# Independent list scatters with waiting readers, and the last block's partial sums loaded ahead

## The chip, the cores and the metric

The kernel runs on one core of one Trainium2 chip. The time is the device time of one execution in microseconds (us); a verdict compares medians of several executions.

## What is computed

Three stages, all in float32, over 2304 tokens of 512 columns: an attention (4 batches, 8 heads, 576 positions, 64 columns a head) with a threshold on the scores; a dense two-layer block with leaky ReLU and 2048 hidden columns; and a mixture of 8 experts in which every token goes to the one expert that its logits choose.

```python
x = attention(q, k, v, tau).transpose(0, 2, 1, 3).reshape(2304, 512)
h = x @ w_in
x = np.maximum(0.01 * h, h) @ w_out
logits = x @ w_gate + modality_bias[modality_id]
e_idx = np.argmax(logits, axis=1)
for e in range(8):
    mask = e_idx == e
    h = np.maximum(x[mask] @ w1[e], 0.0)          # 1024 hidden columns
    out[mask] = gate_w[mask, None] * (h @ w2[e])  # gate_w: the softmax of the chosen logit
```

## The kernel before, in words

A float32 matrix is split into a high and a low part, and a product is three matmuls (high x high, high x low, low x high). The program is one fixed order of instructions for each engine, written out by Python generators; nothing is scheduled by a planner. Each engine works its own row in order, and the framework adds the waits between engines and for DMAs from what reads and writes what.

The attention (0 to about 545 us) works 128 rows at a time; in its gaps the `Units` compute the first 6 of the 16 hidden slices of the dense block for blocks of 256 tokens, and write these partial sums to DRAM (`yp`). There are 9 blocks (`NB`). After the attention, `Tail.run` goes through a list of `items`, each one hidden slice (128 columns) of one block or group: first layer into `h` (L421), activation, and two items later (`LAG` is 2) the second layer into `y` (L453). The items are: slices 0 to 5 of blocks 6 to 8; slices 6 to 15 of the blocks in pairs (0 and 1, 2 and 3, 4 and 5, 6 and 7); slices 6 to 15 of block 8 alone; then two early expert groups of 8 slices each. What has to be done ahead of an item stands in a list `pre` with the item's number at which it falls due: loads of tokens (`fetch`), loads of partial sums (`fetch_part`), transposes (`turn`), and for the early groups `ahead` with the loads of ids and weights, the gather of the group's tokens and the splits of its weights.

When a block's last slice is through, `done1` adds the partial sums to `y` and puts steps for that block into `extra`, of which a few run per item: logits, expert choice and rank (`Route.block`), then three DMAs on POOL: the tokens with their gate to DRAM (`yd`, L604), and two scatters of 128 token numbers each (L606) into `idt`, the lists of the experts. Both scatters write the same DRAM tensor; the framework takes the second as one that overwrites the first, and lets POOL wait for the first to land. For the pairs of blocks the partial sums are loaded ahead into the buffers `xgs`; for block 8 they are loaded in `done1` itself, straight into the buffer of the result.

After 6 blocks `early` picks the first two groups: the 256 first tokens of the two fullest experts. `load_ids` loads a group's numbers from `idt` on SP, `gather` clamps them on VectorE (L881) and lets POOL fetch the token rows (L883) into `xgs`. After block 8, `table` sorts the rest of the tokens into groups of 256 or 384 and singles. `Groups.first` loads the first of these dynamic groups (list L1059 and weights L1075, L1077 on SP, gather L1065 on POOL) while the early groups run; then come dynamic loops over groups, each with the loads for the next.

In the rows, PE is TensorE, DVE VectorE, ACT ScalarE, POOL GpSimd, SP the engine that issues most loads. `h`, `y`, `tp` and `ytp` are accumulators, `w` split weights, `cr`, `ur`, `raw` and `eraw` buffers for raw weights, `g` activations, `exg` the gathered tokens of a dynamic group, `eid` its list.

Of the kernel before, what the change touches and what calls it, by code (L numbers as in the profile page):

```python
# [11 lines left out]
F32 = mybir.dt.float32  # L12
# [443 lines left out]
class Route:  # L456
    def __init__(self, tc, cp, dram, ident, mid, wg, wgt, mb, tmp):
# [10 lines left out]
        self.have = 0  # L468
# [92 lines left out]
    def block(self, b, y, sb, ps, ps_tag):  # L561
# [43 lines left out]
        for t in range(2):  # L605
            nc.gpsimd.indirect_dma_start(out=self.idt, out_offset=IOA(ap=pi[:, t:t + 1], axis=0),  # L606
                                         in_=self.ids[:, 2 * b + t:2 * b + t + 1], in_offset=None)
            yield

# [134 lines left out]
class Tail:  # L744
# [83 lines left out]
    def fetch_part(self, b):  # L828
        for t in range(2):
            self.tc.nc.sync.dma_start(self.xgs[b % 2][:, t, 0:DM], self.mo.yp[2 * b + t])  # L830

    def done1(self, b, ys, part):
        nc = self.tc.nc
        yt = self.yt()
        for t in range(2):
            if part == 2:
                nc.vector.tensor_tensor(yt[:, t, 0:DM], ys[t], self.xgs[b % 2][:, t, 0:DM], op=ALU.add)
            elif part:
                nc.sync.dma_start(yt[:, t, 0:DM], self.mo.yp[2 * b + t])
                nc.vector.tensor_tensor(yt[:, t, 0:DM], ys[t], yt[:, t, 0:DM], op=ALU.add)  # L840
            elif t == 0:
                nc.vector.tensor_copy(yt[:, t, 0:DM], ys[t])
            else:
                nc.scalar.activation(yt[:, t, 0:DM], ys[t], AF.Copy)
# [27 lines left out]
    def load_ids(self, g):  # L872
        assert self.blocks == NB - 3
        base = self.entry(g, 1, NID - GT)
        ids = self.idb()
        self.tc.nc.sync.dma_start(ids, self.rt.idt[ds(base, GT), :].rearrange("(p t) o -> p (t o)", t=2))
        self.ids[g] = ids
# [46 lines left out]
    def ahead(self, g, p):  # L924

        a = [(0, 0, lambda: self.load_ids(g)), (p - 7, 1, lambda: self.gather(g)),
# [103 lines left out]
class Groups:  # L1030
# [25 lines left out]
    def load_ids(self, slot, to, nt=3):  # L1056
        nc = self.nc
        base = nc.sync.value_load(self.rt.slot(1, slot), min_val=0, max_val=NID - TT)
        nc.sync.dma_start(to[:, 0:2], self.rt.idt[ds(base, GT), :].rearrange("(p t) o -> p (t o)", t=2))  # L1059
# [318 lines left out]
def body(tc, qkt, vt, tau, win, wout, mid, wg, wgt, mb, w1, w2, out):  # L1378
    nc = tc.nc
    with ExitStack() as top, tc.manual_schedule():  # L1380
# [73 lines left out]
        def both(b, ys):  # L1454
            for k in range(2):
                ta.done1(b + k, ys[2 * k:2 * k + 2], 2)
# [9 lines left out]
        pre += [(p - 4, 0, 0, lambda: ta.fetch(b))] + [(p - 2 + t, 0, 0, lambda t=t: ta.turn(b, t)) for t in range(2)]  # L1466
        items += [item(b, fi, start=fi == NA, stop=fi == NF - 1, done=(lambda ys: ta.done1(b, ys, 1))) for fi in range(NA, NF)]
# [91 lines left out]
```

## Time and profile before

| | |
|---|---|
| median of 3 runs | 1040.73 us (1039.37 to 1041.92) |
| the profiled execution | 1042.11 us, of it span 1040.3 us |
| TensorE matmul busy | 934.5 us (90%), 7073 instructions |
| weight loads of TensorE | 818.0 us (79%) |
| VectorE busy | 716.6 us (69%) |
| ScalarE busy | 590.6 us (57%) |
| GpSimd busy | 433.6 us (42%) |
| mean granted TensorE clock | 0.958 of full speed |

TensorE is the busiest engine, with an average that mixes stages: some 475 of the first 545 us, nearly all of the time from 545 to 754 us, with gaps between 754 and 811 us, and again nearly all of it until 992 us. The span is counted from the first to the last instruction; what lies around it is 1.8 us. A row that says what an engine waited for names the one event that came last.

### The profile page before, as it was taken

Reading aid. Unit: us, or ns where it says so; the run is one execution under the profiler, and the core shown is the slowest. Engines: PE = TensorE matmul, PEld = TensorE weight load, DVE = VectorE, ACT = ScalarE, POOL = GpSimd, SP = SyncE. Lnnn points to the kernel's source line nnn. Section 1 sums busy time; section 2 is a strip of 40 time slices with the busy share of each in tenths; the row PEclk is TensorE's granted clock in tenths of the full one; section 3 lists DMA queues with packets and bytes.
Section 4 is the critical chain, followed back from the end, with each engine's and each line's share of the span. In section 5 each row is a group of like instructions: output and inputs, shape, how many; then the busy total and the mean of one; then the engine's idle time right before and its main releaser. Section 6 shows DMA issues by size and latency. Waiting matters only on the chain. (4 is left out here: it accounts for less than half of the span.)

```text
span 1040.3 us, 20475 instructions
## 1 busy us (share of the span) xinstructions
PE 934.5 (90%) x7073; PEld 818.0 (79%) x7073; DVE 716.6 (69%) x1749; ACT 590.6 (57%) x1168; POOL 433.6 (42%) x523
## 2 busy tenths in 40 slices
PE   4666779999998998999999999999978999999993
PEld 3565769888897997887887878788967898998962
DVE  7988989889898984776247473844656666565573
ACT  6687878889897874664222222222524555664473
POOL 3899988889888872332001010010122211221120
PEclk7888899999999998999999999999989999999997
DMA  8899999999999986554040220124694987766472
GB/s 214 212 210 255 224 231 205 206 213 240 222 200 216 214 158 181 181 183 142 1 162 20 48 75 20 61 41 143 100 195 135 342 298 260 250 227 202 128 275 104
DMA packets 261721, 181.96 MB, mean 175 GB/s; under 512 B 186258, under 2 KB 223254, under 8 KB 261592
## 3 DMA queue, kind: packets, MB, share of 16 engines
q1 hardware_dynamic: 249248, 155.78, 60.6%
q0 software_dynamic: 6032, 17.68, 5.9%
q10 hardware_dynamic: 6312, 6.94, 2.2%
q8 instruction: 61, 1.00, 0.5%
q14 instruction: 68, 0.56, 0.2%
HBM read 118.88 MB, written 19.79 MB: 133 GB/s over the span
## 5 line engine op out<-in xcount | busy, mean ns | idle before, releaser
L196 POOL TENSOR_TENSOR p<-p,p 128x512 f16<-128x512 f32 x144 | 170.3, 1182 | 0.0
L150 PE MATMUL s<-khh,qs 128*128 128x288 f32 x320 | 104.9, 342 | 49.8 <-DVE p L175 27.9
L453 PE MATMUL y<-w,g 128*128 128x512 f32 x480 | 130.7, 409 | 0.0
L429 ACT ACTIVATE ct<-h 128x256 f32<-128x256 f32 (+1 forms) x104 | 48.5, 466 | 139.7 <-PE h L421 135.2
L158 DVE TENSOR_REDUCE s<-s 128x1 f32<-128x576 f32 x144 | 109.3, 759 | 26.4 <-PE s L223 23.0
L431 DVE SCALAR_TENSOR_TENSOR h<-h,ct 128x256 f32<-128x256 f32 (+1 forms) x104 | 55.2, 531 | 104.8 <-ACT ct L429 104.5
L175 DVE SCALAR_TENSOR_TENSOR p<-s,tb,e 128x576 f32<-128x576 f32 x144 | 117.2, 814 | 8.3 <-ACT e L167 5.2
L421 PE MATMUL h<-w,w 128*128 128x512 f32 x480 | 120.3, 396 | 1.3 <-ACT w L410 0.9
L453 PE MATMUL y<-w,w 128*128 128x512 f32 x480 | 119.2, 395 | 0.0
L222 PE MATMUL s<-vs,pt 128*128 128x128 bf16 (+1 forms) x680 | 109.0, 228 | 5.9 <-DMA pt<-p 5.9
L150 PEld LDWEIGHTS s<-khh,qs 128*128 128x128 f32 x320 | 66.2, 207 | 58.7 <-DVE p L175 18.3
L167 ACT ACTIVATE e<-s,tb 128x576 f32<-128x576 f32 x144 | 107.2, 744 | 4.6 <-DVE tb L162 4.5
L421 PEld LDWEIGHTS h<-w,w 128*128 128x128 f32 x480 | 89.2, 188 | 22.9 <-ACT w L410 1.3
L453 PEld LDWEIGHTS y<-w,w 128*128 128x128 f32 x480 | 88.9, 188 | 19.1
L223 PE MATMUL s<-vs,pt 128*128 128x64 bf16 (+1 forms) x680 | 104.0, 198 | 0.0
L194 ACT ACTIVATE p<-p 128x576 f16<-128x576 f32 x144 | 99.3, 690 | 5.1 <-DVE tb L162 4.2
L453 PEld LDWEIGHTS y<-w,g 128*128 128x128 f32 x480 | 86.2, 192 | 14.6
L150 PE MATMUL s<-kll,qs 128*128 128x288 f32 x320 | 96.4, 315 | 0.0
L421 PE MATMUL h<-uxh,w 128*128 128x256 f32 x448 | 90.5, 300 | 3.2 <-DVE g L440 2.5
L225 PE MATMUL s<-vs,pt 128*128 128x128 bf16 (+1 forms) x544 | 89.8, 226 | 0.0
L421 PE MATMUL h<-exh,w 128*128 128x256 f32 (+1 forms) x448 | 85.8, 288 | 0.7 <-ACT exh L410 0.7
L222 PEld LDWEIGHTS <-pt 128*128 128x128 f16 (+1 forms) x680 | 68.9, 104 | 18.2 <-DMA pt<-p 7.3
(250 smaller groups left out, 2286.7 us busy)
## 6 DMA issues: line engine op xcount, KB each, us to landing
cr<-w SPq DMA_DIRECT2D x36, 512.0 KB
raw_qk<-qkt SPq DMA_DIRECT2D x30, 576.0 KB
raw<-w SPq DMA_DIRECT2D x24, 512.0 KB
eraw<-w SPq DMA_DIRECT2D x18, 512.0 KB
cr<-w_in SPq DMA_DIRECT2D x16, 512.0 KB
cr<-w_out SPq DMA_DIRECT2D x16, 512.0 KB
ur<-xd SPq DMA_DIRECT2D x13, 512.0 KB
ur<-w SPq DMA_DIRECT2D x12, 512.0 KB
```

The source lines that it names most:

```text
L150: nc.tensor.matmul(s[:, j, 0:288], qf[:, c0:c0 + P], x[:, j * 288:(j + 1) * 288], start=(k == 0), stop=(k == len(ops) - 1))
L158: v.tensor_reduce(self.mq[n], self.sq[n], axis=AX.XY, op=ALU.min)
L167: self.tc.nc.scalar.activation(e, self.sq[n], AF.Exp, bias=self.mq[n][:, 1:2], scale=-1.0)
L175: self.tc.nc.vector.scalar_tensor_tensor(p, self.sq.pop(n), self.mq.pop(n)[:, 0:1], self.eq.pop(n), op0=ALU.is_le, op1=ALU.mult, accum_out ...
L194: nc.scalar.activation(pp[:, 0:S], p, AF.Copy)
L196: nc.gpsimd.tensor_tensor(pp[:, S + D:], p[:, 0:4 * P], pp[:, 0:4 * P], op=ALU.subtract)
L222: nc.tensor.matmul(o[r0:r1, 0:2 * D], hi, v12, start=(c == 0), stop=False)
L223: nc.tensor.matmul(o[r0:r1, D:2 * D], hi, vs[:, h, c, 2], start=False, stop=(c == 4))
L225: nc.tensor.matmul(o[r0:r1, 0:2 * D], pt[:, 5 + c, r0:r1], v12, start=False, stop=False)
L421: nc.tensor.matmul(h, w[:, 0, a, s], b[:, c], start=(n == 0), stop=(n == 11))
L431: nc.vector.scalar_tensor_tensor(h, h, 0.01, a, op0=ALU.mult, op1=ALU.max)
L453: nc.tensor.matmul(y, a[:, s], w[:, 1, b], start=start and k == 0, stop=stop and k == 2)
```

## The change

Four edits. `fetch_part` and `done1`: block 8's partial sums go into the buffer `xgs[1]` too, by an entry in `pre` due five items into block 8, and `done1` has one form for all blocks. `Route.block`: the 18 scatters are declared to be independent of one another, their names are kept in `put`, and a memset of one column follows each on POOL. `listed`: the loads of lists in `load_ids` (both of that name) wait for all scatters issued so far. `ahead`: a group's gather is due one item later.

```diff
@@ -465,7 +465,8 @@
         nc.scalar.dma_start(bs, mb.rearrange("(o m) e -> o m e", o=1).to_broadcast([P, 2, E]))
         mi = tmp[4].bitcast(I32)[:, 0:36].rearrange("p (t w) -> p t w", w=2)
         nc.scalar.dma_start(mi, mid.bitcast(I32).rearrange("(t p) w -> p t w", p=P))
-        self.have = 0
+        self.have, self.put = 0, []
+        self.gap = cp.tile([P, 1], F32, name="gap")
         self.consts = self.prepare(nc, cp, dram, tmp, bs, mi)
 
     def prepare(self, nc, cp, dram, tmp, bs, mi):
@@ -603,9 +604,19 @@
         v.tensor_copy(pi, pf)
         nc.gpsimd.dma_start(self.yd[b * GT:(b + 1) * GT, :].rearrange("(t p) c -> p t c", t=2), y)
         for t in range(2):
-            nc.gpsimd.indirect_dma_start(out=self.idt, out_offset=IOA(ap=pi[:, t:t + 1], axis=0),
-                                         in_=self.ids[:, 2 * b + t:2 * b + t + 1], in_offset=None)
+            i = nc.gpsimd.indirect_dma_start(out=self.idt, out_offset=IOA(ap=pi[:, t:t + 1], axis=0),
+                                             in_=self.ids[:, 2 * b + t:2 * b + t + 1], in_offset=None)
+            self.tc.declare_no_dep(i.ins, group="idt", reason="every token has its own place in the lists")
+            self.tc.add_to_no_dep_group("idt", i.ins)
+            self.put.append(i.ins.name)
+            nc.gpsimd.memset(self.gap, 0.0)
             yield
+
+    def listed(self, dma):
+
+        for name in self.put:
+            self.tc.add_manual_dep(dma.ins, name, mybir.DependencyInfo(mybir.DependencyClass.Sync, mybir.DependencyReason.DATA))
+        self.put = []
 
     def early(self, sb):
 
@@ -826,22 +837,15 @@
             self.tc.nc.scalar.dma_start(self.mo.yp[2 * b + t], o)
 
     def fetch_part(self, b):
+        to = self.xgs[b % 2 if b < NB - 1 else 1]
         for t in range(2):
-            self.tc.nc.sync.dma_start(self.xgs[b % 2][:, t, 0:DM], self.mo.yp[2 * b + t])
-
-    def done1(self, b, ys, part):
+            self.tc.nc.sync.dma_start(to[:, t, 0:DM], self.mo.yp[2 * b + t])
+
+    def done1(self, b, ys):
         nc = self.tc.nc
         yt = self.yt()
         for t in range(2):
-            if part == 2:
-                nc.vector.tensor_tensor(yt[:, t, 0:DM], ys[t], self.xgs[b % 2][:, t, 0:DM], op=ALU.add)
-            elif part:
-                nc.sync.dma_start(yt[:, t, 0:DM], self.mo.yp[2 * b + t])
-                nc.vector.tensor_tensor(yt[:, t, 0:DM], ys[t], yt[:, t, 0:DM], op=ALU.add)
-            elif t == 0:
-                nc.vector.tensor_copy(yt[:, t, 0:DM], ys[t])
-            else:
-                nc.scalar.activation(yt[:, t, 0:DM], ys[t], AF.Copy)
+            nc.vector.tensor_tensor(yt[:, t, 0:DM], ys[t], self.xgs[b % 2 if b < NB - 1 else 1][:, t, 0:DM], op=ALU.add)
         if self.blocks == 0:
             self.rt.load_wide(self.raws[2:])
         self.blocks += 1
@@ -873,7 +877,7 @@
         assert self.blocks == NB - 3
         base = self.entry(g, 1, NID - GT)
         ids = self.idb()
-        self.tc.nc.sync.dma_start(ids, self.rt.idt[ds(base, GT), :].rearrange("(p t) o -> p (t o)", t=2))
+        self.rt.listed(self.tc.nc.sync.dma_start(ids, self.rt.idt[ds(base, GT), :].rearrange("(p t) o -> p (t o)", t=2)))
         self.ids[g] = ids
 
     def gather(self, g):
@@ -923,7 +927,7 @@
 
     def ahead(self, g, p):
 
-        a = [(0, 0, lambda: self.load_ids(g)), (p - 7, 1, lambda: self.gather(g)),
+        a = [(0, 0, lambda: self.load_ids(g)), (p - 6, 1, lambda: self.gather(g)),
              (p - 2, 3, lambda: self.turn_g(g, 0)), (p - 1, 3, lambda: self.turn_g(g, 1))]
         def load(q):
             def load():
@@ -1056,7 +1060,7 @@
     def load_ids(self, slot, to, nt=3):
         nc = self.nc
         base = nc.sync.value_load(self.rt.slot(1, slot), min_val=0, max_val=NID - TT)
-        nc.sync.dma_start(to[:, 0:2], self.rt.idt[ds(base, GT), :].rearrange("(p t) o -> p (t o)", t=2))
+        self.rt.listed(nc.sync.dma_start(to[:, 0:2], self.rt.idt[ds(base, GT), :].rearrange("(p t) o -> p (t o)", t=2)))
         if nt == 3:
             nc.sync.dma_start(to[:, 2:3], self.rt.idt[ds(base + GT, P), :])
 
@@ -1453,7 +1457,7 @@
 
         def both(b, ys):
             for k in range(2):
-                ta.done1(b + k, ys[2 * k:2 * k + 2], 2)
+                ta.done1(b + k, ys[2 * k:2 * k + 2])
         for b in range(0, NB - 1, 2):
             p = len(items)
             for k in range(2):
@@ -1463,8 +1467,8 @@
                       for fi in range(NA, NF)]
         items[(NB - len(FB)) * NA]["hook"] = lambda: bank.__setitem__(0, lambda: None)
         b, p = NB - 1, len(items)
-        pre += [(p - 4, 0, 0, lambda: ta.fetch(b))] + [(p - 2 + t, 0, 0, lambda t=t: ta.turn(b, t)) for t in range(2)]
-        items += [item(b, fi, start=fi == NA, stop=fi == NF - 1, done=(lambda ys: ta.done1(b, ys, 1))) for fi in range(NA, NF)]
+        pre += [(p - 4, 0, 0, lambda: ta.fetch(b)), (p + 5, 0, 0, lambda: ta.fetch_part(b))] + [(p - 2 + t, 0, 0, lambda t=t: ta.turn(b, t)) for t in range(2)]
+        items += [item(b, fi, start=fi == NA, stop=fi == NF - 1, done=(lambda ys: ta.done1(b, ys))) for fi in range(NA, NF)]
         p = len(items)
         for g in range(2):
             items += ta.group(g, (lambda g, ys: groups().after(g)) if g else ta.done2)
```

The engines' rows, before and after. In them `DMASW` is a semaphore of the DMAs that POOL issues, `DMAHW` of those that SP and ACT issue, and the others belong to the engines; `yd` is the store of a block's tokens, `idt` a scatter into the lists, `pi` the places that it writes.

POOL from block 7's store on, before:

```order
L604 DMA yd<-yt_92 128x2x516 [waits DVE_49]
L606 DMA idt<-ids,pi 20480x1 [waits DMASW6_49,DVE_49]
L606 DMA idt<-ids,pi 20480x1 [waits DMASW0_49]
L883 DMA xg_7110<-yd,ids_7108 128x516 [waits DMAHW5_49,DMASW2_49,DVE_49]
L883 DMA xg_7110<-yd,ids_7108 128x516 [waits DMAHW6_49,DMASW3_49]
L1046 IOTA eid_9864 128x3 [waits PE_49,Pool_49]
L604 DMA yd<-yt_91 128x2x516 [waits DMASW4_49,DVE_49]
L606 DMA idt<-ids,pi 20480x1 [waits DMASW1_49,DVE_49]
L606 DMA idt<-ids,pi 20480x1 [waits DMASW5_49]
```

and now:

```order
L605 DMA yd<-yt_92 128x2x516 [waits DVE_49]
L607 DMA idt<-ids,pi 20480x1 [waits DMASW0_49,DVE_49]
L612 MEMSET gap 128x1 [waits Pool_49]
L607 DMA idt<-ids,pi 20480x1 [waits DMASW1_49]
L612 MEMSET gap 128x1 [waits Pool_49]
L1050 IOTA eid_9878 128x3 [waits PE_49]
L887 DMA xg_7111<-yd,ids_7109 128x516 [waits DMAHW6_49,DMASW2_49,DVE_49]
L887 DMA xg_7111<-yd,ids_7109 128x516 [waits DMAHW7_49,DMASW3_49]
L605 DMA yd<-yt_91 128x2x516 [waits DMASW4_49,DVE_49]
L607 DMA idt<-ids,pi 20480x1 [waits DMASW5_49,DVE_49]
L612 MEMSET gap 128x1 [waits Pool_49]
L607 DMA idt<-ids,pi 20480x1 [waits DMASW6_49]
```

The second scatter of a block waited for a semaphore of the first (`DMASW0` for block 7, `DMASW5` for block 8); it now waits for that of the DMA eight places before it on POOL, a scatter two blocks older, or for none. The second early group's gather stays behind block 7's scatters, and the iota of the dynamic groups goes ahead of it.

VectorE around block 8's addition (`yt` from `y`), before:

```order
L447 TENSOR_TENSOR w_73<-cr_89,w_73 128x512 [waits Activation_49]
L447 TENSOR_TENSOR w_73<-cr_90,w_73 128x512 [waits Activation_49]
L881 TENSOR_SCALAR ids_7108<-ids_7106 128x2 [waits DMAHW1_49]
L840 TENSOR_TENSOR yt_91<-y_7113,yt_91 128x512 [waits DMAHW4_49,DMASW4_49,PE_49]
L840 TENSOR_TENSOR yt_91<-y_7114,yt_91 128x512 [waits DMAHW5_49,PE_49]
L1047 MEMSET egate 128x3
L440 SCALAR_TENSOR_TENSOR g<-h_7111,g 128x256 [waits Activation_49]
L447 TENSOR_TENSOR w_7088<-ur,w_7088 128x512 [waits DMAHW0_49,Activation_49]
L447 TENSOR_TENSOR w_7088<-raw_7099,w_7088 128x512 [waits DMAHW1_49,Activation_49]
```

and now:

```order
L447 TENSOR_TENSOR w_73<-cr_89,w_73 128x512 [waits Activation_49]
L447 TENSOR_TENSOR w_73<-cr_90,w_73 128x512 [waits Activation_49]
L848 TENSOR_TENSOR yt_91<-y_7114,xg_7111 128x512 [waits DMAHW6_49,DMASW4_49,PE_49]
L848 TENSOR_TENSOR yt_91<-y_7115,xg_7111 128x512 [waits DMAHW7_49,PE_49]
L1051 MEMSET egate 128x3
L440 SCALAR_TENSOR_TENSOR g<-h_7112,g 128x256 [waits Activation_49]
L447 TENSOR_TENSOR w_7089<-ur,w_7089 128x512 [waits DMAHW2_49,Activation_49]
L447 TENSOR_TENSOR w_7089<-raw_7100,w_7089 128x512 [waits DMAHW3_49,Activation_49]
L885 TENSOR_SCALAR ids_7109<-ids_7107 128x2
```

The clamp of the second early group's numbers (`ids`) moves from ahead of the addition to behind the next item's weight splits, and the addition reads `xg` in place of its own result buffer.

SP among the first early group's weight loads, before:

```order
L895 DMA raw_7099<-w 128x2x512 [waits DMAHW3_49]
L893 ISA
L893 DMA raw_7100<-w 128x4x256 [waits DMAHW4_49,DVE_49]
L895 ISA
L895 DMA cr_88<-w 128x2x512 [waits DMAHW5_49,DVE_49,Activation_49]
L893 ISA
L893 DMA cr_89<-w 128x4x256 [waits DMAHW6_49,DVE_49,Activation_49]
L895 ISA
L895 DMA cr_90<-w 128x2x512 [waits DVE_49]
```

and now:

```order
L899 DMA raw_7100<-w 128x2x512 [waits DMAHW3_49]
L897 ISA
L897 DMA raw_7101<-w 128x4x256 [waits DMAHW4_49,DVE_49]
L899 ISA
L899 DMA cr_88<-w 128x2x512 [waits DMAHW5_49,DVE_49,Activation_49]
L842 DMA xg_7111<-yp 128x512 [waits DMAHW6_49,DVE_49]
L842 DMA xg_7111<-yp 128x512 [waits DVE_49]
L897 ISA
L897 DMA cr_89<-w 128x4x256 [waits DMAHW0_49,Activation_49]
L899 ISA
L899 DMA cr_90<-w 128x2x512 [waits DMAHW1_49]
```

The two loads of partial sums (`xg` from `yp`) stand here now, between the fourth and the fifth weight load, and wait for VectorE; they stood (into `yt`, L839) behind the tenth weight load of the two early groups, where one weight load now follows the other.

## Rows read from the trace of the kernel before

**Rows 1.** Busy time of each engine by stretch, with TensorE's clock, DMA share and GB/s.

```profile
754.50:762.10 7.60, 5.14 (x27) 4.55 (x27) 4.38 (x9) 2.15 (x5) 0.31 (x1) 0.78 1.06 276
770.00:779.70 9.70, 5.20 (x28) 4.64 (x27) 3.90 (x13) 2.13 (x5) 1.82 (x2) 0.82 0.60 135
799.70:810.30 10.60, 5.70 (x26) 5.14 (x26) 5.23 (x9) 4.70 (x10) 1.29 (x2) 0.68 1.01 355
830.00:995.00 165.00, 161.60 (x995) 144.75 (x993) 95.79 (x173) 89.79 (x179) 31.41 (x30) 1.00 0.66 223
```

**Rows 2.** Timeline of PE: start us, us, engine, line, operation, idle before and its end.

```profile
736.61 0.60 PE L405 MATMUL tp<-ident,xg 128*128 128x128 f32 x4
...
751.64 1.55 PE L453 MATMUL y<-w,g 128*128 128x512 f32 x6
...
754.47 1.54 PE L453 MATMUL y<-w,g 128*128 128x512 f32 x6
758.46 0.80 PE L421 MATMUL h<-uxh,w 128*128 128x256 f32 x2 [2.46 <-DVE g L440]
...
762.12 1.63 PE L453 MATMUL y<-w,g 128*128 128x512 f32 x6
...
774.51 0.63 PE L405 MATMUL tp<-ident,xg 128*128 128x128 f32 x4 [4.50 <-issue]
...
779.33 0.60 PE L405 MATMUL tp<-ident,xg 128*128 128x128 f32 x4
779.69 1.64 PE L453 MATMUL y<-w,g 128*128 128x512 f32 x6
...
804.61 1.08 PE L405 MATMUL tp<-ident,exg 128*128 128x128 f32 x4 [4.90 <-DMA exg<-yd,eid]
...
810.34 4.43 PE L453 MATMUL y<-w,g 128*128 128x512 f32 x18
```

**Rows 3.** Timeline of DVE.

```profile
713.79 2.73 DVE L837 TENSOR_TENSOR yt<-y,xg 128x512 f32<-128x512 f32 x4
...
751.22 0.16 DVE L881 TENSOR_SCALAR ids<-ids 128x2 int32<-128x2 int32 x1
756.76 1.31 DVE L840 TENSOR_TENSOR yt<-y,yt 128x512 f32<-128x512 f32 x2 [5.38 <-DMA yt<-yp]
...
788.39 0.21 DVE L703 TENSOR_SCALAR tab<-tw,tgv 128x1 int32<-128x1 f32 x1
```

**Rows 4.** Timeline of SP's DMA queue.

```profile
744.48 0.85 SPq L839 DMA_DIRECT2D yt<-yp  x2
...
795.09 0.35 SPq L1059 DMA_DIRECT2D eid<-idt  x1
```

**Rows 5.** Timeline of POOL.

```profile
721.23 0.99 POOL L883 DMA_INDIRECT xg<-yd,ids  x1 [22.08 <-DVE ids L881]
...
753.83 0.98 POOL L606 DMA_INDIRECT idt<-ids,pi  x1 [4.05 <-DMA idt<-ids,pi]
764.80 0.96 POOL L606 DMA_INDIRECT idt<-ids,pi  x1 [9.99 <-DMA idt<-ids,pi]
766.07 0.99 POOL L883 DMA_INDIRECT xg<-yd,ids  x1 [0.30 <-DVE oh L577]
...
770.11 0.79 POOL L604 DMA_DIRECT2D yd<-yt  x1 [1.60 <-DVE pf L601]
...
786.89 0.97 POOL L606 DMA_INDIRECT idt<-ids,pi  x1 [10.82 <-DMA idt<-ids,pi]
```

**Rows 6.** Waits of POOL and of SP's queue: total us, times, longest.

```profile
POOL idt L606 <- DMA idt<-ids,pi: 49.7, 7, 10.8
...
SPq L1059 <- DMA idt<-ids,pi: 5.2, 1, 5.2
```

**Rows 7.** Page, DMA issues: count, median us from issue to landing.

```profile
exg<-yd,eid POOLq DMA_INDIRECT x24, 6.3
idt<-ids,pi POOLq DMA_INDIRECT x18, 7.9
```

## The prediction

> **What bounds the kernel now.** I read the waits first, then TensorE's timeline where it waits, then the queues that it waits for. From 830 to 995 us PE is busy for 161.6 of 165 us at full clock [rows 1], and the dynamic groups there follow one another on PE: whatever PE gains before 810 us moves all of that forward by as much. So the question is where PE stands still between the last shared block and the first dynamic group. It does so three times. At 758.46 it has waited 2.46 us, at 774.51 4.50 us, at 804.61 4.90 us [rows 2]. Behind each wait the clock falls: the three stretches show a mean granted clock of 0.78, 0.82 and 0.68 of 2.4 GHz [rows 1], the engine having done nothing for 2.5 to 5 us and then running at the lower level.
>
> What each wait really costs is read from start to start. Two second-layer groups of one item stand 2.83 us apart (751.64, 754.47), four transposes cost 0.36 us (779.33 to 779.69) [rows 2]. One item with two sets of transposes is therefore 2.83 + 2 x 0.36 = 3.55 us undisturbed. Measured:
> - first, 754.47 to 762.12: 7.65, of it lost 4.10;
> - second, from the idle's start 774.51 - 4.50 = 770.01 to 779.69: 9.68, lost 6.13;
> - third, 804.61 - 4.90 = 799.71 to 810.34: 10.63, lost 7.08.
>
> Together 17.31 us, of which 11.86 are waits and 5.45 slow clock.
>
> Who is late each time: (1) VectorE's addition of block 8's partial sums, which stood 5.38 us for their load [rows 3]; the load left SP at 744.48 [rows 4] and so took 12 us. PE waits since the release of its h buffer is queued behind that addition on VectorE. (2) The gather of the second early group, issued at 766.07, though VectorE had its indices ready at 751.22 [rows 3, 5]: on POOL it stands behind block 7's second scatter, which waited for the first (753.83, 764.80) [rows 5]. Its data let PE go on at 774.51, 8.44 us after the issue. (3) The gather of the first dynamic group, whose list SP could load only at 795.09, 5.2 us late [rows 4, 6], because block 8's second scatter had waited 10.82 us for the first and left at 786.89 [rows 5].
>
> **The change part by part.**
>
> *Partial sums ahead.* The two loads (256 KB each) go from their place at 744.48 to a place behind the first four weight loads; there SP waits for block 7's addition, and two weight loads of the first group stand behind it. That addition ends at 713.79 + 2.73 = 716.5 [rows 3]; with the 12 us of the load at 744.48 the two weight loads land by 729, the group's first transposes run at 736.61 [rows 2], and these are its fifth and sixth slices of eight. So this costs nothing; without that cover it would be what the landing is late. Block 8's addition then starts when VectorE reaches it, right after 751.22 + 0.16 instead of 756.76 [rows 3], and the buffer release comes 5.4 us sooner, against 2.46 us of PE's wait. The first loss goes whole: -4.10. Next late there is nothing until PE meets the transposes of the second group, at 770.01 - 4.10 = 765.91.
>
> *Scatters without waits.* POOL stood 49.7 us for seven of the waits after 680 us [rows 6]; only those that hold back a gather or a list cost PE anything. The 18 added memsets write one column each; no row shows their like, and from above I bound one by the 1.27 us of a DMA issue (764.80 to 766.07, rows 5), from below by the 0.30 us that POOL leaves between two issues. Either way they lie on an engine that waits for its next work, and count only between the last two scatters. The waits that the framework puts in their place are for the DMA eight places earlier on POOL; for block 8's second scatter that is block 6's second scatter, long landed.
>
> *Gather one item later.* Index clamp and gather of both early groups move by one item, 2.83 us. The first goes from 721.23 to about 724.1 and with 8.44 us lands at 732.5; PE wants it at 736.61 [rows 2, 5]: covered by 4. The second: clamp at 751.22 + 2.83 = 754.05, POOL's iota ahead of it waits only for matmuls that are over, issue near 754.6. By 8.44 us it lands at 763.0, by the slowest scatter (10.82 + 1.0 = 11.8 us, rows 5) at 766.4. PE arrives at 765.91: idle 0 to 0.5. Second loss gone: -6.13, to -5.6 at worst.
>
> *The last lists.* Block 8's store goes out at 770.11 - 4.10 = 766.0, and POOL issues one DMA per 1.27 us (764.80 to 766.07) [rows 5]: scatters at 767.3 and, behind a memset, 768.9 (to 769.8). No row shows two scatters in flight. From below their landing is bounded by the median of 7.9 us [rows 7], from above by 11.8: 776.8 to 781.6. SP also needs the table, which VectorE finishes at 788.39 [rows 3]; with 10.23 us saved, at 778.16. In the profile 795.09 - 5.2 - 788.39 = 1.5 us pass from there until SP could load, so the list is loaded between 779.7 and 781.6. From that load to PE's transposes it is 804.61 - 795.09 = 9.52 us: 789.2 to 791.1. PE arrives at 799.71 - 10.23 = 789.48. So the wait is 0 to 1.6 us; I take the lower landing time, since the loads of that moment are over by then, and charge 0.5 us for both gathers together. Third loss: -7.08.
>
> Sum: -4.10 - 6.13 - 7.08 + 0.5 = -16.8 us. The profiled execution took 1042.11 us, 1.8 outside its span of 1040.3: 1025.3 by it. The median of the runs, 1040.73, lies 1.4 below; from it 1023.9, say 1024.
>
> **The rivals.**
>
> A. *The lists land late.* Two scatters and block 8's store in flight share the DMA engines with weight loads, and the list load is delayed by each us that the last scatter needs beyond 11.8. What PE gains in all is then 795.09 less the list load's new time, and the slow clock behind the wait, 10.63 - 3.55 - 4.90 = 2.2 us, stays. At 1.5 times 11.8 the last lands at 786.6: gain 8.5, 1032. At twice that, 792.5: gain 2.6, 1038. For it: the first scatter of block 8 took those 11.8 us beside loads, against a median of 7.9 [rows 5, 7]. The Trainium skill (DMA: Bandwidth & Descriptors, Queues, rings and completion order) says that each DMA engine takes turns between the queues that have work, packet by packet; the trace's 7.9 against 11.8 fits that, and by it a scatter beside 1 MB of loads stays slow. Against it: the loads of that time are 1 MB, and the profile's last scatter ran after them.
>
> B. *The gain is used up on the way*: the first dynamic group's weight loads stand behind the list load on SP, or the last stage hangs on transfers that do not start sooner. Then 1038 to 1043. Against it: those loads are issued behind the same list load, which comes 15 us sooner, and 161.6 of 165 us are PE's [rows 1].
>
> C. *Slower: POOL's queue works its transfers off one by one.* The wait was then no cost; only its place changes, and gathers and store now stand behind scatters on the queue itself. From 753.83 - 4.05 = 749.8 two scatters at 7.9 to 11.8 and a gather at 8.44 end at 774 to 782 (now 774.5); the second gather and two scatters, the store not counted, bring the last list to 798 to 814, where 795.09 is the point from which the kernel gets slower: 3 to 19 us, 1044 to 1060, middle 1052. The Trainium skill (DMA: Bandwidth & Descriptors, SWDGE vs HWDGE vs iDMA) says that only one software queue is allocated; its section Two DMAs through the same engine are not ordered says that descriptors of a queue start in order but overlap, which is the case against. In the trace: the 24 gathers, issued in threes, land in a median of 6.3 us [rows 7], where a third in a row would need three times that.
>
> **How the numbers follow.** Forecast 0.68 (1022 to 1026: the losses gone but for 0 to 2 us, and the spread of the runs). A 0.20, of it three quarters up to 1032. B 0.06. C 0.06. From 1022 to 1032 some 0.8 is held: low end 1039.4, the fastest run, less 17.3; high end A at 1.5 times the slowest scatter. A measurement of this kernel can tell about 0.3%, 3 us: faster 0.88 (forecast and A), the same 0.06 (B), slower 0.06 (C).
>
> **What would show it.** In the profile of the changed kernel: no wait of VectorE for partial sums and none of PE near 756; block 7's and 8's scatter pairs 1.3 to 1.5 us apart on POOL; the second early gather near 754.6; the list of the first dynamic group loaded near 780, right behind the table; the granted clock at 1.00 through the three stretches; PE busy time per stage unchanged. If PE still waits more than 2 us at the third place, A is right and the scatters' landing time was mis-sized; if the gathers land behind the scatters by their sum, C.

## The result, and the profile after

The changed kernel took 1031.85 us (median of 4 runs, 1029.97 to 1032.68) beside 1040.05 for the kernel before (4 runs, 1039.15 to 1041.92): ratio 0.9915, 95% interval 0.9893 to 0.9937. It is faster, by 8.2 us where 16.8 had been worked out, and 0.15 us inside the upper end of the range. The profiled execution has a span of 1030.1 us, 10.2 less than before.

The three stretches first. Busy time of each engine by stretch in the changed kernel, with TensorE's clock, DMA share and GB/s, to be held against [rows 1]:

```profile
759.50:763.20 3.70, 3.70 (x29) 3.43 (x27) 1.72 (x3) 2.26 (x5) 2.40 (x2) 1.00 1.22 82
770.80:774.50 3.70, 3.70 (x29) 3.43 (x28) 3.07 (x10) 2.12 (x5) 2.87 (x4) 1.00 0.95 289
789.40:800.00 10.60, 10.60 (x69) 9.58 (x68) 6.46 (x12) 6.57 (x14) 1.91 (x2) 1.00 1.04 362
820.00:985.00 165.00, 161.48 (x987) 144.81 (x985) 95.37 (x172) 88.59 (x178) 31.42 (x30) 0.99 0.65 221
```

In all three PE is busy from end to end at a granted clock of 1.00, that is 2.4 GHz; before it was 0.78, 0.82 and 0.68. Timeline of PE at those places, answering [rows 2]:

```profile
759.48 1.56 PE L453 MATMUL y<-w,g 128*128 128x512 f32 x6
...
763.12 1.65 PE L453 MATMUL y<-w,g 128*128 128x512 f32 x6
...
770.86 0.60 PE L405 MATMUL tp<-ident,xg 128*128 128x128 f32 x4
...
774.49 1.63 PE L453 MATMUL y<-w,g 128*128 128x512 f32 x6
...
794.99 0.60 PE L405 MATMUL tp<-ident,exg 128*128 128x128 f32 x4
...
798.62 4.45 PE L453 MATMUL y<-w,g 128*128 128x512 f32 x18
```

No row shows an idle time before it. From one second-layer group to the next it is 763.12 - 759.48 = 3.64 us where it was 7.65 (undisturbed: 3.55), and the first dynamic group starts without a wait. The timelines of VectorE, POOL and SP's queue show why, answering [rows 3 to 5]:

```profile
756.20 1.28 DVE L848 TENSOR_TENSOR yt<-y,xg 128x512 f32<-128x512 f32 x2
```

```profile
755.07 1.48 POOL L607 DMA_INDIRECT idt<-ids,pi  x1 [0.30 <-DVE g L440]
756.85 0.96 POOL L607 DMA_INDIRECT idt<-ids,pi  x1 [0.19 <-issue]
759.48 1.03 POOL L887 DMA_INDIRECT xg<-yd,ids  x1 [1.47 <-DVE ids L885]
...
772.21 1.01 POOL L607 DMA_INDIRECT idt<-ids,pi  x1 [0.30 <-DVE g L440]
773.52 1.34 POOL L607 DMA_INDIRECT idt<-ids,pi  x1 [0.19 <-issue]
```

```profile
784.95 0.35 SPq L1063 DMA_DIRECT2D eid<-idt  x1
```

The addition does not wait for its partial sums, the scatters of a pair leave 1.3 to 1.8 us apart instead of 11 to 12, and the list is loaded at 784.95 instead of 795.09. What it was last waiting for is in the waits of SP's queue, where [rows 6] had 5.2 us for the scatter:

```profile
SPq L1062 <- DVE tab L714: 13.2, 1, 13.2
```

The table on VectorE was the last to come, not the scatters into the lists. So all that the prediction looked for is there. All of it is about 5 us later in the span than it should be, though, and the lateness is already complete at the first block's store on POOL, before the first instruction that the change touches. Before, and then after:

```profile
560.67 0.94 POOL L604 DMA_DIRECT2D yd<-yt  x1 [68.84 <-DVE pi L603]
```

```profile
565.70 0.94 POOL L605 DMA_DIRECT2D yd<-yt  x1 [68.86 <-DVE pi L604]
```

The books of the two profiled executions: the first stage lost 565.70 - 560.67 = 5.03 us; from there to the first dynamic group (810.34 before, 798.62 after) 11.72 + 5.03 = 16.75 us were gained; from that group to the end of the span 1.5 us were lost (229.96 before, 231.48 after). -16.75 + 5.03 + 1.5 = -10.2. The gain stands there as forecast. The question was what had cost 5 us in a stage whose instructions are the same, in the same order, on every engine.

### The profile page after: what moved, and what is told of

Same layout as the page of the kernel before. It is cut to its first block, busy times and chain, and to the rows that moved or that the text cites. A ratio compares the mean times of both kernels' runs of the same rounds, so it can differ in the third digit from the quotient of the medians.

```text
span 1030.1 us, 20493 instructions
## 1 busy us (share of the span) xinstructions
PE 930.9 (90%) x7073; PEld 814.2 (79%) x7073; DVE 715.5 (69%) x1749; ACT 589.8 (57%) x1168; POOL 437.4 (42%) x541
## 5 line engine op out<-in xcount | busy, mean ns | idle before, releaser
L222 PE MATMUL s<-vs,pt 128*128 128x128 bf16 (+1 forms) x680 | 107.7, 227 | 9.4 <-DMA pt<-p 9.4
L605 POOL DMA_DIRECT2D yd<-yt x9 | 7.0, 780 | 203.6 <-DVE pf L602 134.7
L225 PE MATMUL s<-vs,pt 128*128 128x128 bf16 (+1 forms) x544 | 88.8, 225 | 0.0
```

What stands on the lines that cost most here:

```text
L222: nc.tensor.matmul(o[r0:r1, 0:2 * D], hi, v12, start=(c == 0), stop=False)
L225: nc.tensor.matmul(o[r0:r1, 0:2 * D], pt[:, 5 + c, r0:r1], v12, start=False, stop=False)
```

## The experiments

One thing does differ there: the new tile of one column moves every tile allocated behind it by 32 bytes (so I read the allocation; no row shows an address). That was my first theory; its rival was that the stage just differs from execution to execution. Each kernel was run beside the kernel before on the same chip (its time is in the table); the rest is the span from the first block's store to the end, from the profiled execution.

| kernel | time, us (runs) | kernel before beside it (runs) | ratio, 95% interval | first store | rest |
|---|---|---|---|---|---|
| before, first profile | 1040.73 (3) | | | 560.67 | 479.6 |
| changed, first profile | 1031.85 (4) | 1040.05 (4) | 0.9915 (0.9893 to 0.9937) | 565.70 | 464.4 |
| before, tiles 32 bytes on | 1050.03 (12) | 1047.52 (23) | 1.0022 (0.9999 to 1.0046) | 562.45 | 481.0 |
| before, 64 bytes on | 1047.22 (12) | 1047.52 (23) | 0.9998 (0.9968 to 1.0027) | 564.75 | 485.4 |
| changed, 64 bytes on | 1027.91 (6) | 1047.52 (23) | 0.9812 (0.9778 to 0.9846) | 563.40 | 464.1 |
| changed, no new tile | 1029.43 (6) | 1047.52 (23) | 0.9833 (0.9796 to 0.9871) | 559.58 | 462.9 |
| changed, again | 1030.47 (6) | 1047.20 (11) | 0.9832 (0.9793 to 0.9871) | 564.30 | 465.8 |
| changed, no new tile, again | 1029.18 (6) | 1047.20 (11) | 0.9816 (0.9777 to 0.9855) | 564.76 | 464.4 |
| scatters, gather an item later | 1030.82 (6) | 1047.20 (11) | 0.9841 (0.9805 to 0.9877) | 560.51 | 466.5 |
| scatters alone | 1027.60 (6) | 1048.05 (17) | 0.9809 (0.9785 to 0.9834) | 560.27 | 465.8 |
| sums ahead, gather an item later | 1042.52 (12) | 1048.05 (17) | 0.9966 (0.9944 to 0.9988) | 561.30 | 478.5 |
| changed, block 8's pair chained | 1037.53 (6) | 1048.05 (17) | 0.9905 (0.9878 to 0.9933) | 562.54 | 472.5 |
| changed, block 7's pair chained | 1040.22 (6) | 1048.05 (17) | 0.9927 (0.9900 to 0.9954) | 563.80 | 479.3 |

**Where the tiles lie.** Four kernels; in all four every instruction but the memsets stands where it stood.

```diff
 (the kernel before, tiles 32 bytes on; with 16 for 1: 64 bytes on)
+        self.gap = cp.tile([P, 1], F32, name="gap")
+        nc.gpsimd.memset(self.gap[:, 0:1], 0.0)
 (the changed kernel, 64 bytes on)
-        self.gap = cp.tile([P, 1], F32, name="gap")
+        self.gap = cp.tile([P, 16], F32, name="gap")
...
-            nc.gpsimd.memset(self.gap, 0.0)
+            nc.gpsimd.memset(self.gap[:, 0:1], 0.0)
 (the changed kernel, no new tile)
-        self.gap = cp.tile([P, 1], F32, name="gap")
...
-            nc.gpsimd.memset(self.gap, 0.0)
+            nc.gpsimd.memset(self.zr[:, 0:1], 0.0)
```

> The kernel before, plus the changed kernel's one-column tile in the constants, written once at the start and never read. Every instruction of every engine stays in its order, one memset on POOL apart; what changes is that each tile allocated behind it lies 32 bytes further on in its partition. Theory P (place): the changed kernel's late first stage comes from that shift. Then this kernel is late by the same 5.03 us: first block store of the rows at 565.7 us of the span instead of 560.67, time 1040.05 + 5 = about 1045. Theory N (no matter of place: the 5 us are chance of an execution, or come from the added waits): first store at 560.7, time 1039 to 1041.

> The kernel before, plus a tile of 16 columns in the constants, its first column written once: the same as the first of these runs, with a shift of 64 bytes. Theory P by the remainder by 64: no loss, first store at 560.7 us, 1039 to 1041. Theory P with any shift: 565.7 and about 1045. Theory N: 1039 to 1041.

> The changed kernel with the tile 16 columns wide instead of one, the memset on its first column as before: the tiles behind it lie 64 bytes further on than in the kernel before, and are multiples of 64 again. Theory P, if it is the remainder by 64 that counts: the first stage is back at its old time, first store of the rows at 560.7, the rest as in the changed kernel, 1031.85 - 5 = about 1026.8. If any shift costs, as the changed kernel: 565.7 and 1031.9. Theory N: 1030 to 1032.7, the changed kernel's own spread.

> The changed kernel without the new tile: the same memsets write one column of the tile of zeros that is there already (4 partitions), and all tiles lie where they lay in the kernel before. Order of all instructions as in the changed kernel. Theory P: first store at 560.7 us, no PE wait at the three places, about 1026.8 us, which would be faster than both kernels and 2.8 us above the forecast of 1024. Theory N: 565.7 as in the changed kernel or anything between, 1030 to 1032.7.

Measured: with the tiles 32 bytes on the kernel before is not told apart from itself (1.0022, 0.9999 to 1.0046), and its first store is at 562.45 instead of 565.7; 64 bytes on it is at 564.75. In the changed kernel it is at 563.40 with 64 bytes and at 559.58 without a shift. The stores do not go by the shift. The 23 runs of the kernel before in this group, one program on one chip, reach from 1043.19 to 1052.09. What no theory had expected: beside them the two forms of the changed kernel are 17 to 20 us faster, more than the forecast, not less.

So the next two runs put the changed kernel, word for word, beside the one without the tile.

> The changed kernel itself, word for word, beside the next kernel on one chip. Theory P (the 32 bytes by which its tiles lie further on cost its first stage 5 us): slower than the next kernel by 3 to 5 us, first block's store near 565. Theory V (the first stage takes longer or shorter from execution to execution, as the 43 runs of the last call do on one chip, from 1043.2 to 1052.1 for the kernel before): same as the next kernel within 2 us, and against the kernel before of the same call a gain of 15 to 19 us, not the 8.2 first measured.

> The changed kernel with its memsets on a tile that is there already, so that all tiles lie as in the kernel before, once more, beside the changed kernel on one chip. Theory P: faster than the changed kernel by 3 to 5 us. Theory V: within 2 us of it; a gain of 15 to 19 us against the kernel before of the same call.

Measured: 1030.47 and 1029.18, ranges 1027.28 to 1034.75 and 1026.41 to 1032.57, first store at 564.30 and 564.76. The theory of the 32 bytes has fallen as a cause of 5 us; 2 us or so of it could hide in the spread. Against the kernel before the changed kernel now gains 0.0168 x 1047.2 = 17.6 us (13.5 to 21.7). In the 14 profiles (the table's 13 and one below) the first store lies anywhere from 559.58 to 565.70, and the two profiles that the result was first read from happen to be near the two ends. The change does not move it: its mean is 562.9 in the five profiles with all scatters chained and 562.8 in the nine others.

**Which part brings it.** The partial sums ahead, first without any other edit:

```diff
-        pre += [(p - 4, 0, 0, lambda: ta.fetch(b))] + [ ...
+        pre += [(p - 4, 0, 0, lambda: ta.fetch(b)), (p + 5, 0, 0, lambda: ta.fetch_part(b))] + [ ...
...
-                nc.sync.dma_start(yt[:, t, 0:DM], self.mo.yp[2 * b + t])
-                nc.vector.tensor_tensor(yt[:, t, 0:DM], ys[t], yt[:, t, 0:DM], op=ALU.add)
+            nc.vector.tensor_tensor(yt[:, t, 0:DM], ys[t], self.xgs[b % 2 if b < NB - 1 else 1][:, t, 0:DM], op=ALU.add)
```

> The kernel before with the last block's partial sums loaded ahead, and nothing else of the change; no new tile. Since the runs so far put the first block's store anywhere from 559.6 to 564.8 us whatever lies where, the rest of the span, from that store to the end, is counted too: 479.6 in the kernel before, 464.4 in the changed kernel. If the three losses add up as the prediction has it, the first alone goes: -4.10, rest 475.5. If they are chained, PE meets at the second place the same gather, still issued at about 766.1 and landing at 774.5 since it hangs on block 7's scatters and not on PE: the second wait grows from 4.50 to about 8.6 us and eats the gain; block 8's store and scatters leave POOL some 2.8 us sooner, since they came behind its rows: rest 476.8 to 479.6, that is 0 to -2.8 against the kernel before of the same call.

Measured: 1059.23 us (6 runs; before 1047.20), 1% slower, first store at 565.38. This kernel changes the computation: written in this order, the second early gather fills the buffer of block 8's partial sums before the addition has read them, and the addition takes the gathered rows instead. Timelines of POOL and VectorE in it:

```profile
770.83 0.99 POOL L876 DMA_INDIRECT xg<-yd,ids  x1 [0.30 <-issue]
```

```profile
781.23 1.38 DVE L837 TENSOR_TENSOR yt<-y,xg 128x512 f32<-128x512 f32 x2 [25.13 <-issue]
```

VectorE stands 25.13 us, until 10.40 us after that gather's issue. Nothing follows from it on the price of the part. What follows is why the diff moves the gather by an item: without that the loads ahead have no free buffer. So with both:

```diff
 (the edit above, and)
-        a = [(0, 0, lambda: self.load_ids(g)), (p - 7, 1, lambda: self.gather(g)),
+        a = [(0, 0, lambda: self.load_ids(g)), (p - 6, 1, lambda: self.gather(g)),
```

> The kernel before with the last block's partial sums loaded ahead and the early gathers one item later, so that the second one can't overwrite those sums before the addition has read them; scatters in a chain as before, no new tile. Theory S (a chain sets the time): the second early gather stands on POOL behind block 7's second scatter, 764.80 in the kernel before, and block 8's scatters behind that one's landing, whatever PE gains ahead of them. VectorE's wait for the sums goes, PE's first wait with it, and PE stands at the second place until the same 774.5: its wait there is about 8.6 us instead of 4.50, the last list leaves SP no sooner, and the time is that of the kernel before of the same call within 2 us (rest of the span from the first block's store 479.6 to 485, where the kernels with chained scatters have it so far). By the prediction's sum the part is worth 4.10 us: 4 us below the kernel before of the same call, rest 475.5 to 481.

Timelines of VectorE, POOL and PE:

```profile
751.89 1.28 DVE L837 TENSOR_TENSOR yt<-y,xg 128x512 f32<-128x512 f32 x2
```

```profile
768.88 0.96 POOL L606 DMA_INDIRECT idt<-ids,pi  x1 [10.99 <-DMA idt<-ids,pi]
770.18 1.04 POOL L876 DMA_INDIRECT xg<-yd,ids  x1 [0.17 <-issue]
```

```profile
778.69 1.08 PE L405 MATMUL tp<-ident,xg 128*128 128x128 f32 x4 [12.06 <-issue]
...
784.76 1.64 PE L453 MATMUL y<-w,g 128*128 128x512 f32 x6
...
804.76 0.63 PE L405 MATMUL tp<-ident,exg 128*128 128x128 f32 x4
```

Measured: 0.0034 x 1048 = 3.6 us faster (1.3 to 5.9). The time is what the sum said, the way is not. The addition's wait is gone and PE's first with it, but the second gather still stands behind block 7's scatter, and PE now waits 12.06 us for it instead of 4.50. (`issue` says that the profile names no event for this wait; these transposes read the gather's rows, and the profile's list of DMA issues gives 8.4 us from issue to landing for that gather in the kernel before, whose transposes ran 8.44 us after it.) Since it arrives later at the third place, it finds its rows there. By the measure of [rows 2] the first loss went (-4.10), the second grew from 6.13 to 14.58 (778.69 - 12.06 = 766.63, to the group at 784.76, less 3.55: +8.45), and the third went (-7.08): -2.73. So the losses are not prices that add up: the second and the third are one late chain of scatters, which PE meets at one place or at the other.

Then the scatters without the partial sums: the changed kernel without its new tile, with the last addition's loads as before, first with the gather an item later, then also with the gather in its old place (the two edits above, taken back one after the other).

> The changed kernel with the last block's partial sums loaded as in the kernel before, in the addition's place, and its memsets on a tile that is there already, so that all tiles lie as before. The independent scatters, their readers' waits and the gather one item later stay. By the prediction's sum the first wait of 2.46 us near 756 comes back with its slow clock (4.10 us), and the second and the third stay away: 13.2 us less than the kernel before of the same call, rest of the span from the first block's store 466 to 468. If the first loss had been swallowed by a later one, nothing comes back: as the kernel with both parts, 463 to 464.5.

> Independent scatters and their readers' waits alone: partial sums loaded in the addition's place and early gathers where they stood before, no new tile. Against the kernel with the gathers one item later (rest 466.5; there PE waited 0.29 us for the first and 1.39 us for the second) the second gather need no longer come behind the addition on VectorE: its indices are ready near 749, it leaves POOL near 753 behind block 7's scatters and lands near 762, 4 us ahead of PE. Then the second wait goes, rest 464 to 465.5, and the whole gain of the change is that of the scatters: 15 to 18 us below the kernel before of the same call. If the gather beside the load of the sums slows that load, PE's first wait grows to 1 to 2.5 us instead, rest 466 to 469.

Timelines of the second, scatters alone: VectorE, POOL, PE.

```profile
753.74 1.33 DVE L850 TENSOR_TENSOR yt<-y,yt 128x512 f32<-128x512 f32 x2 [2.57 <-DMA yt<-yp]
```

```profile
749.72 1.48 POOL L606 DMA_INDIRECT idt<-ids,pi  x1 [0.30 <-DVE g L440]
751.50 0.96 POOL L606 DMA_INDIRECT idt<-ids,pi  x1 [0.22 <-issue]
752.76 0.99 POOL L893 DMA_INDIRECT xg<-yd,ids  x1 [0.23 <-issue]
754.06 0.97 POOL L893 DMA_INDIRECT xg<-yd,ids  x1 [0.30 <-issue]
```

```profile
765.69 0.63 PE L405 MATMUL tp<-ident,xg 128*128 128x128 f32 x4
...
769.00 0.60 PE L405 MATMUL tp<-ident,xg 128*128 128x128 f32 x4
...
790.67 0.63 PE L405 MATMUL tp<-ident,exg 128*128 128x128 f32 x4 [0.72 <-DMA exg<-yd,eid]
```

Measured: scatters alone are 20.0 us faster than before (17.4 to 22.5), with the gather later 16.7 (12.9 to 20.4). The whole gain of the change is the scatters'; the other two edits bring nothing that shows here. With the gather later the rest, 466.5, lies where the first loss coming back would put it, but PE waits 0.29 us at the first place and 1.39 us at the second, where the gather's clamp now stands behind the addition on VectorE: the number fits, the way does not. The first loss, which had been put on the partial sums' late issue, went without that being touched. Their load, issued at 744.64, is there when the addition starts at 753.74, 9.1 us later instead of 12.28; the addition waits 2.57 us instead of 5.38, and PE no longer waits for what is behind it. The load is the same and left at the same time; what stands around it is not. Busy time by stretch for the middle of the load in the kernel before, the last two columns being DMA share and GB/s:

```profile
748.50:755.50 7.00, 7.00 (x45) 6.30 (x45) 2.31 (x9) 3.62 (x8) 1.74 (x2) 1.00 0.73 97
```

and for the whole load with scatters alone:

```profile
744.60:753.80 9.20, 9.20 (x66) 8.23 (x65) 5.28 (x22) 4.49 (x10) 4.35 (x6) 1.00 1.00 348
```

97 GB/s against 348; over the whole load, 744.48 to 756.76, the kernel before moved 175. In the kernel before block 6's second scatter, issued at 741.38, was in flight over that stretch (the next one, which waits for it, left at 753.83 [rows 5]); with scatters alone it left at 733.27. It does not take the partial sums. With the sums ahead and all scatters chained, where that scatter left at 743.04, the two weight loads of this place (744.00, 744.60) meet the same: 124 GB/s from 747.00 to 754.00. In the last kernel below, where block 6's pair is independent and its second scatter left at 736.78, the same two loads (747.07, 747.67) run at 332 GB/s over the same stretch behind their issue, 750.07 to 757.07. That the late scatter itself slows the loads is the nearest reading, but these runs don't separate it from other traffic of that moment: with scatters alone block 7's pair is in flight beside the load too, at 749.72 and 751.50, and there the load keeps its rate.

**One wait put back at a time.** In the changed kernel without the new tile, one scatter is taken out of the group of independent ones:

```diff
-            self.tc.declare_no_dep(i.ins, group="idt", reason="every token has its own place in the lists")
-            self.tc.add_to_no_dep_group("idt", i.ins)
+            if not (t and b == NB - 1):
+                self.tc.declare_no_dep(i.ins, group="idt", reason="every token has its own place in the lists")
+                self.tc.add_to_no_dep_group("idt", i.ins)
 (second kernel: b == NB - 2)
```

> The changed kernel, memsets on a tile that is there already, with one wait put back: block 8's second scatter waits again for its first. All else as in the changed kernel, whose rest of the span is 462.9 to 465.8. By the prediction's sum the third loss comes back, 7.08 us: rest 471.4. Worked out along the chain: the second scatter leaves POOL some 10.8 us behind the first instead of 1.3, the list is loaded 8.2 us behind it, about 7.3 us later than in the changed kernel, PE waits 6.7 us at the first dynamic group and loses 2.2 us of clock behind that: 8.9 us, rest 473. If this wait was covered by the table on VectorE (ready about 778) or anything else: no change, 463 to 466.

POOL and PE with block 8's pair chained:

```profile
769.01 1.01 POOL L606 DMA_INDIRECT idt<-ids,pi  x1 [0.30 <-DVE g L440]
780.31 1.02 POOL L606 DMA_INDIRECT idt<-ids,pi  x1 [10.20 <-DMA idt<-ids,pi]
```

```profile
799.22 1.09 PE L405 MATMUL tp<-ident,exg 128*128 128x128 f32 x4 [6.90 <-DMA exg<-yd,eid]
```

Measured: a wait of 6.90 us at the first dynamic group (expected 6.7), rest 472.5 (expected 473 along the chain, 471.4 by the prediction's sum), against a mean of 464.3 for the five profiles of the changed kernel: 8.2 us for one wait of one scatter.

> The same with the other wait put back: block 7's second scatter waits for its first; block 8's pair stays independent. By the prediction's sum the second loss comes back, 6.13 us: rest 470.4. Along the chain: the scatter leaves POOL about 766 instead of 756.9, the gathers behind it at 767.3, their rows land at 775.7, PE, there at 770.9, waits 4.9 us and loses 1.6 us of clock: 6.5 us, rest 470.8; block 8's scatters come behind that one's landing at about 775, its list near 787, and PE, late by 6.5 us itself, doesn't wait for it. If the loss is swallowed at the third place: 463 to 466.

POOL and PE with block 7's pair chained:

```profile
753.23 1.48 POOL L606 DMA_INDIRECT idt<-ids,pi  x1 [0.30 <-DVE g L440]
767.00 0.96 POOL L606 DMA_INDIRECT idt<-ids,pi  x1 [12.21 <-DMA cr<-w]
768.33 1.03 POOL L887 DMA_INDIRECT xg<-yd,ids  x1 [0.17 <-issue]
```

```profile
780.92 1.08 PE L405 MATMUL tp<-ident,xg 128*128 128x128 f32 x4 [11.83 <-issue]
...
807.70 0.63 PE L405 MATMUL tp<-ident,exg 128*128 128x128 f32 x4 [0.94 <-DMA exg<-yd,eid]
```

Measured: a wait of 11.83 us at the second place, where 4.9 were expected, rest 479.3 instead of 470.8. (The profile names a weight load as the scatter's releaser. In the changed kernel this scatter waits for no weight load, and the one wait that was put back is that for the first scatter, so I take it for that.) The place is right, the size isn't: the scatter leaves 13.77 us behind the first (10.97 in [rows 5]) and the gather's rows release PE 12.6 us after its issue (8.44 before). The profiled execution is the longest of this kernel's six (1044.84, median 1040.22); by the medians the wait costs 1040.22 - 1027.60 = 12.6 us beside scatters alone on that chip. The two waits put back singly cost 8.2 and 15.0 us by the rests, more together than the 17.7 between the two kernels (482.0, the mean of the three profiles with all scatters chained and the sums in their old place, less 464.3).

## Why the prediction was right, and where it was not

**The mechanism held.** PE's three waits went with their slow clock, and what was gained up to the first dynamic group is 16.75 us in the two first profiles, where the steps had said 17.3 less 0.5. Beside each other on one chip the kernels are 17.6 us apart (13.5 to 21.7), which holds the 16.8.

**The bounds of the unknown costs.** The memsets cost nothing that shows, less than the lower bound of 0.30 us: their rows last 0.11 to 0.12 us and lie in the 0.30 us that POOL leaves between two issues anyway. The scatters of a pair are 1.3 to 1.8 us apart, block 8's 1.31, where the steps had 1.6 to 2.5 and the list of signs 1.3 to 1.5. The gather comes 193.78 us behind the first store, the forecast's 754.6 being 193.9. The list comes 219.25 behind it, forecast 219.0 to 220.9. SP was held by the table alone at the end, so the landing of two scatters in flight, for which 11.8 us had been the upper bound, took at most 784.95 - 773.52 = 11.4.

**The step that failed for the measured time** is one that was not written: everything ahead of 700 us was taken over from one profiled execution, and its spread put at that of three runs, 1039.4 to 1041.9. The first stage differs by up to 6.1 us between executions, whatever the change. In the first two profiles this took 5.03 of the 16.75 us. Up to the first block's store PE's waits sum to 69.9 us before and 73.6 after, among them 8.2 and 18.1 for the attention's transposed tiles (`pt` from `p`, by DMA; 5.3 to 15.0 in the other twelve profiles); why they differ stays open. Of the 1.5 us lost behind the third place 1.34 are in one stretch of the dynamic groups. From the transposes at 956.20 before and at 944.57 after to those of the next group it is 28.96 and 30.30 us; in both PE has waited 1.11 us and waits 0.69 us more, but the granted clock of the stretch is 1.00 before and 0.94 after. In five other profiles with independent scatters the stretch takes 28.94 to 28.95 us, so this too belongs to the execution.

**What was luck.** That is the account of two executions and not of the medians, since the other first runs have no profile. By the medians the changed kernel stays where it was (1031.85, later 1030.47), and it is the kernel before that lies elsewhere (1040.05, later 1047.20). The first measurement is small because the kernel before was fast in it, and why it was is open. The 1031.85 lie 0.15 us inside the range, whose upper end had been put there for rival A. A did not happen, so the range held this time in part by luck.

**A second step failed without moving the sum:** the losses were priced place by place, each with its own cause. The edit against the first one, the earlier issue of the partial sums, was not needed at all: with scatters alone the loss is gone. What was read as that load's own duration, 12 us, was its duration in that traffic. And single losses can't be booked singly: sums ahead with the scatters chained make the second wait 12.06 us, one chained pair alone costs 8.2 or 15.0.

**The rivals.** A (lists late): no; SP waited for the table. With block 8's pair chained the list comes 225.9 us behind the first store instead of 219.25, and PE waits 6.90 us for what follows: this place has little to spare. C (POOL's queue one by one): no; with scatters alone two scatters and two gathers start on POOL between 749.72 and 754.06, and PE's transposes of the gathered rows run without a wait at 765.69 and 769.00, 16.0 and 19.3 us after the first scatter's issue. One by one, two scatters at 7.9 us and the gathers at 6.3 [rows 7] would need 22.1 and 28.4. The Trainium skill (DMA: Bandwidth & Descriptors, Two DMAs through the same engine are not ordered) says that descriptors of one queue start in order but overlap; these rows agree.

**What is open:** why the kernel before took 1039 to 1042 us in the first 4 runs and 1042.5 to 1052.8 in 51 later ones, on three chips, while the changed kernel lies at a median of 1031.85 in its first runs and of 1030.47 in the later ones. The profiles give a part. With chained scatters the second gather leaves POOL 205.4, 208.0 and 207.7 us behind the first store (the kernel before and its two shifted forms) and the rest is 479.6, 481.0 and 485.4; in the changed kernel it leaves 193.78 and 193.84 us behind it (first profile, and again without the tile), the list 219.25 and 219.20, and the five rests lie within 2.9 us. A chain of landing times varies with each of them; computed indices do not. That the kernel before met short landings in its first runs would fit, but of that time only one execution has a profile, and the chip of those runs is not on record.

## What to carry to other kernels

A wait that an unneeded order puts between small scatters can cost as much as a scatter takes to land and more (here 8.2 and 15.0 us for two such waits put back singly), in the queue of an engine on which gathers and list loads depend, and it turns up under other names: as a late load, a late gather, a late list. Take the chain out before its symptoms, and price the waits along the chain, not place by place. Before a gain of under 2% is read from two profiles, compare the stretch that the change can't touch in both; here it hid 5 of 16.75 us. And measure the kernel before again in other runs: its median moved by 7 us.

## What was not expected of the hardware

- The same instructions in the same order reach the first block's store between 559.58 and 565.70 us in 14 profiled executions, and moving the tiles by 32 or 64 bytes in their partition is not what decides it; an effect of up to 2 us is not excluded.
- The kernel before reaches from 1043.19 to 1052.09 us in 23 runs on one chip, nearly 1%; three runs had shown a spread of 0.25%.
- A stretch of 7 us with DMA engines busy for 0.73 of the time moved 97 GB/s, and two loads of 256 KB in flight over it took 12.28 us (175 GB/s over all of it), against 9.1 us with 348 GB/s where block 6's second scatter had left 8 us sooner. Why is not shown.
